# Linear attention on one core: stores behind loads, eps matmuls of 32 rows, head 0 in halves, a new order of work

## The chip, the cores and the metric

The kernel runs on one core of a Trainium2 chip. The metric is the device time of one execution in microseconds (us), lower is better. Repeated runs of one kernel mostly lie within 0.5% of their median. The span that a profile shows is about 1.8 us shorter than the time of the same run.

The engines are called PE or TensorE (matmul; PEld is its weight load), DVE or VectorE, ACT or ScalarE, and POOL or GpSimd. The sync engine SP issues the transfers (DMA).

## The reference

```python
B, H, S, D = 1, 32, 2048, 128          # q, k, v in bfloat16
phi_q = where(q > 0, q + 1, exp(q)) + 1e-6
phi_k = where(k > 0, k + 1, exp(k)) + 1e-6
kv  = einsum("bhsd,bhse->bhde", phi_k, v)
z   = einsum("bhsd->bhd", phi_k)
num = einsum("bhqd,bhde->bhqe", phi_q, kv)
den = einsum("bhqd,bhd->bhq", phi_q, z)[..., None] + 1e-6
return num / den
```

The kernel writes phi(x) as the sum of two parts, min(exp(x), 1) + 1e-6 and relu(x), and lets TensorE add the two by accumulating a matmul of each. A column of ones beside v gives z with kv, so that one 128x129 result per tile holds a numerator and its denominator.

## The kernel before

Each head h has these named pieces of work. Every engine runs its pieces in a fixed order that is written in the program:

- `ek`, `eq`: exp of k and of the transposed q, on ACT. `em`, `emq`: min with 1 and + 1e-6, on VectorE.
- `rk`: relu of k, on VectorE. `rqa`, `rqb`: relu of q, half on ACT and half on VectorE. In every fourth head (`RELU_Q = "SSSA"`) ACT does it all.
- `v1`: a copy of v beside the column of ones, on POOL. `T`: 16 transposes of q on TensorE.
- `kx`, `kv`: 32 matmuls for kv, and `kvs`: its copy from PSUM by ACT.
- `nB`, `nA`, `nC`: the numerator and denominator, 32 matmuls in six PSUM banks, two banks to a group.
- `rA`, `fA`, `rC`, `fC`: reciprocal and multiply on VectorE, 12 tiles and 4 tiles. Then the store.

The 1e-6 in the denominator (called eps here) comes from one small matmul for each bank. A matrix of ones times three columns that sum to eps opens the bank's accumulation:

```python
def numerator(e, h, tiles):                       # one bank: two or three tiles
    s = h % 2
    e.matmul(_ap(o_ps[:, :], SLOT[tiles[0]] + D, [[NC, len(tiles)]]), lhsT=ones[:], rhs=epsr[:, 0:len(tiles)],
             start=True, stop=False, skip_group_check=True)
    for t in tiles:
        o = o_ps[:, SLOT[t]:SLOT[t] + NC]
        e.matmul(o, lhsT=emq_sb[:, s, t * P:(t + 1) * P], rhs=kvs_sb[:, s, :], start=False, stop=False, ...)
        ins = e.matmul(o, lhsT=rq_sb[:, s, t * P:(t + 1) * P], rhs=kvs_sb[:, s, :], start=False, stop=True, ...)
    return ins
# ... cut ...
# num(which, h, banks): for b in banks: numerator(e, h, BANKS[b])
```

Loads and stores are issued in one order by SP. There are eight input buffers and six output buffers:

```python
NI = 8; NO = 6; LAG = 2
for h in range(NH + LAG - 1):
    if h + NI < NH:
        loads(h + NI)
    if h >= LAG:
        store(h - LAG)
```

## Time and profile before

| | before |
|---|---|
| time, median | 180.02 us (3 runs, 179.67 to 180.59; 180.22 with a fourth, timed beside the changed kernel) |
| span of the profiled run | 177.9 us |
| busy: PE, DVE, ACT | 163.9, 155.8, 161.2 us |
| multiply of 12 tiles (`fA`): head 3 to head 23 | 38.52 to 136.78 us, 4.91 us a head |

The first view is the head of the profile's page: busy time, share of the span and instructions of each engine.

```profile
span 177.9 us, 6326 instructions
PE 163.9 (92%) x2822; PEld 157.7 (89%) x2822; DVE 155.8 (88%) x230; ACT 161.2 (91%) x140; POOL 33.1 (19%) x37
```

The second view is the table of busy time by stretch. A line gives the stretch and its length in us, then busy us (and instructions) of PE, PEld, DVE, ACT and POOL, the granted TensorE clock, the DMA share (a sum of packet times, which can come out above 1) and GB/s.

```profile
0.00:20.00 20.00, 15.20 (x201) 14.43 (x202) 8.52 (x20) 13.15 (x11) 2.93 (x8) 0.91 0.91 346
40.00:140.00 100.00, 99.13 (x1762) 96.13 (x1759) 97.57 (x139) 99.75 (x84) 20.82 (x20) 1.00 1.03 415
```

In the middle three engines and the DMA are all nearly full. Which of them binds is told by the chain of waits, the work that ended last followed back step by step. These are its pieces from 59 to 65 us (start, length, what):

```profile
58.92 1.77 ACT la L394
60.69 0.91 ACT la L399
61.60 0.17 ACT la L373
61.77 1.80 ACT la L347
63.57 1.77 ACT la L394
```

The chain runs through ACT without a gap: exp of k (L347), exp of q (L394), half a relu (L399), the copy of kv (L373). That is 4.65 us a head, and 5.5 where ACT does the whole relu. From 40 to 140 us ACT makes up 71% of the chain; VectorE has 13%, and one wait for an outgoing transfer 14%. PE's busy figure of 99% is no evidence of a bound. The records of matmuls overlap: those of full ones are 0.22 us long but start 0.05 to 0.06 us apart, as the timeline of TensorE at an eps matmul (L277) shows:

```profile
60.63 0.22 PE L281 MATMUL la<-la 128*128 128x129 bf16 x1
60.68 0.22 PE L283 MATMUL la<-la 128*128 128x129 bf16 x1
60.74 0.17 PE L277 MATMUL la<-la 128*128 128x3 bf16 x1
60.77 0.22 PE L281 MATMUL la<-la 128*128 128x129 bf16 x1
```

The weight loads (PEld) of the same matmuls follow each other as closely, the one for the eps matmul too:

```profile
60.63 0.10 PEld L283 LDWEIGHTS la<-la 128*128 128x128 bf16 x1
60.69 0.10 PEld L277 LDWEIGHTS la<-la 128*128 128x128 bf16 x1
60.74 0.10 PEld L281 LDWEIGHTS la<-la 128*128 128x128 bf16 x1
```

Read the starts and not the lengths. A full matmul takes 0.057 us from start to start, an eps matmul 0.03. By starts TensorE needs 1.85 us (kv) + 0.89 (transposes) + 1.97 (numerator with six eps matmuls) = 4.7 us a head, which is 0.2 less than the 4.9 us that a head takes.

### The profile page before, as it was taken

To read this page: it belongs to the slowest core of one execution; us is meant where nothing else is said; L and a number is where in the kernel's file an instruction comes from. 1 tells how busy PE (TensorE), PEld (TensorE's weight loads), DVE (VectorE), ACT (ScalarE), POOL (GpSimd) and SP (SyncE) were. 2 spreads that over 40 slices of the span, in tenths; PEclk is the share of its full clock that TensorE was granted. 3 is DMA by queue.
4 is the path that set the end of the run, shared out by engine and by line. 5 is a ranking of instruction groups with operands and counts; after the bars stand their busy time and mean duration, and the time that the engine had idled before them with its cause. 6 is when DMAs were issued, how large, how long until landed. Compare 5 with 4: busy or idle time off the path is not lost.

```text
span 177.9 us, 6326 instructions
## 1 busy us (share of the span) xinstructions
PE 163.9 (92%) x2822; PEld 157.7 (89%) x2822; DVE 155.8 (88%) x230; ACT 161.2 (91%) x140; POOL 33.1 (19%) x37
## 2 busy tenths in 40 slices
PE   6849987999999999999999999999999899999981
PEld 6848886999999999999998999989999799999971
DVE  1255699799999999999999999999999899999983
ACT  5396999989999999999999999999999989996572
POOL 1022022222121222222121122222222022222000
PEclk9996999999999999999999999999999999999998
DMA  5999999999999999999999999999999999984336
GB/s 156 366 417 412 410 407 411 406 410 404 414 415 416 416 413 416 418 412 421 414 411 420 415 418 416 415 419 415 415 416 415 420 413 420 411 333 179 125 122 236
DMA packets 18891, 67.52 MB, mean 380 GB/s; under 512 B 2096, under 2 KB 2480, under 8 KB 18864
## 3 DMA queue, kind: packets, MB, share of 16 engines
q1 hardware_dynamic: 18720, 66.99, 93.7%
q8 instruction: 22, 0.36, 0.8%
q10 hardware_dynamic: 144, 0.13, 0.2%
q14 instruction: 5, 0.04, 0.1%
HBM read 50.33 MB, written 16.78 MB: 377 GB/s over the span
## 4 chain that ended last, share of the span: by engine, by line
ACT 48%; PE 20%; DVE 16%; DMA 12%; issue 1%; SPq 0%; DVEq 0%
ACT la L347 19%; ACT la L394 18%; PE la L362 9%; DMA out_dram<-la 9%; ACT la L399 8%; DVE la L307 8%; PE la L281 4%; PE la L283 3%; PE la L354 3%; DMA la<-in_q_dram 3%; ACT la L373 2%; DVE la L339 2%; DVE la L402 2%; DVE la L406 2%; DVE la L303 1%
## 5 line engine op out<-in xcount | busy, mean ns | idle before, releaser
L307 DVE TENSOR_TENSOR la<-la 128x512 bf16<-128x512 f32 (+2 forms) x64 | 77.2, 1206 | 3.7 <-DMA out_dram<-la 1.2
L283 PE MATMUL la<-la 128*128 128x129 bf16 x512 | 68.0, 220 | 0.0
L281 PE MATMUL la<-la 128*128 128x129 bf16 x512 | 68.0, 219 | 0.0
L362 PE MATMUL la<-la 128*128 128x129 bf16 x1024 | 65.5, 222 | 0.6 <-DVE la L307 0.5
L394 ACT ACTIVATE la<-la 128x2048 bf16<-128x2048 bf16 x31 | 58.8, 1895 | 5.1 <-PE la L354 3.0
L347 ACT ACTIVATE la<-la 128x2048 bf16<-128x2048 bf16 (+1 forms) x33 | 61.7, 1877 | 1.4 <-DMA la<-in_k_dram 1.4
L362 PEld LDWEIGHTS la<-la 128*128 128x128 bf16 x1024 | 61.3, 99 | 1.2 <-DVE la L307 0.8
L378 POOL COPY la<-la 128x1024 int32<-128x1024 int32 x31 | 32.4, 1046 | 128.7 <-DVE la L303 115.1
L283 PEld LDWEIGHTS la<-la 128*128 128x128 bf16 x512 | 49.5, 97 | 0.0
L281 PEld LDWEIGHTS la<-la 128*128 128x128 bf16 x512 | 47.1, 97 | 0.0
L399 ACT ACTIVATE la<-la 128x1024 bf16<-128x1024 bf16 (+1 forms) x31 | 38.5, 1241 | 0.0
L277 PE MATMUL la<-la 128*128 128x3 bf16 (+1 forms) x192 | 32.5, 169 | 5.1 <-DVE la L307 3.0
L354 PE MATMUL la<-la 128*128 128x128 bf16 x512 | 33.9, 219 | 3.0 <-DVE la L402 2.1
L354 PEld LDWEIGHTS la<-la 128*128 128x128 bf16 x512 | 29.6, 98 | 4.4 <-DVE la L402 3.2
L277 PEld LDWEIGHTS la<-la 128*128 128x128 bf16 x192 | 18.7, 97 | 9.1 <-DVE la L307 7.1
L406 DVE TENSOR_SCALAR la<-la 128x2048 bf16<-128x2048 bf16 x31 | 21.1, 682 | 5.8 <-ACT la L394 5.8
L339 DVE TENSOR_SCALAR la<-la 128x4096 bf16<-128x4096 bf16 (+1 forms) x18 | 19.8, 1100 | 3.0 <-DMA la<-in_k_dram 3.0
L331 DVE TENSOR_SCALAR la<-la 128x4096 bf16<-128x4096 bf16 (+1 forms) x18 | 19.8, 1098 | 1.0 <-ACT la L347 0.9
L402 DVE TENSOR_SCALAR la<-la 128x1024 bf16<-128x1024 bf16 x24 | 16.1, 673 | 2.1 <-ACT la L394 2.1
L303 DVE RECIPROCAL la<-la 128x4 f32<-128x4 f32 (+2 forms) x66 | 13.1, 200 | 2.9 <-PE la L283 2.6
L373 ACT ACTIVATE la<-la 128x129 bf16<-128x129 f32 x32 | 9.6, 301 | 3.1 <-PE la L362 1.6
L437 PE MATMUL la<-la 128*128 128x120 bf16 x70 | 6.2, 273 | 1.5 <-POOL la L222 1.5
(18 smaller groups left out, 16.1 us busy)
## 6 DMA issues: line engine op xcount, KB each, us to landing
la<-in_q_dram SPq DMA_DIRECT2D x32, 512.0 KB, 15.4
la<-in_v_dram SPq DMA_DIRECT2D x32, 512.0 KB, 15.8
la<-in_k_dram SPq DMA_DIRECT2D x31, 512.0 KB, 15.3
out_dram<-la SPq DMA_DIRECT2D x31, 512.0 KB, 15.2
la<-in_k_dram SPq DMA_DIRECT2D x2, 256.0 KB, 2.9
out_dram<-la SPq DMA_DIRECT2D x2, 192.0 KB, 2.1
out_dram<-la ACTq DMA_DIRECT2D x1, 128.0 KB, 1.9
```

What stands on the lines that cost most here:

```text
L277: e.matmul(_ap(o_ps[:, :], SLOT[tiles[0]] + D, [[NC, len(tiles)]]), lhsT=ones[:], rhs=epsr[:, 0:len(tiles)], start=True, stop=False, skip_ ...
L281: e.matmul(o, lhsT=emq_sb[:, s, t * P:(t + 1) * P], rhs=kvs_sb[:, s, :], start=False, stop=False, skip_group_check=True)
L283: ins = e.matmul(o, lhsT=rq_sb[:, s, t * P:(t + 1) * P], rhs=kvs_sb[:, s, :], start=False, stop=True, skip_group_check=True)
L307: add("DVE", f"f{which}{h}", lambda e: e.tensor_tensor(out=_ap(o_sb[:, :, :, :], ob + t0 * D, [[n * D, nb], [D, n], [1, D]]), in0=_ap(o_ps ...
L339: add("DVE", key, lambda e: e.tensor_scalar(rk_sb[:, s:s + n], k_sb[:, b:b + n], 0.0, None, op0=ALU.max), [d for i in range(n) for d in ld ...
L347: add("ACT", "ek0.0" if h == 0 and r == 0 else f"ek{h}", lambda e, c=c: e.activation(em_sb[:, h % 4, c], k_sb[:, h % NI, c], ACT.Exp), ([f ...
L354: ins = e.transpose(xT[:, j * P:(j + 1) * P], q_sb[:, h % NI, j * D:(j + 1) * D], ident[:])
L362: ins = e.matmul(kv_ps, lhsT=src[:, h % 4, j * D:(j + 1) * D], rhs=v1_sb[:, h % 2, j, 0:NC], start=(j + part == 0), stop=(j == NT - 1 and ...
L378: add("DVE" if h < V1_DVE else "POOL", f"v1{h}", lambda e, h=h, s=s: e.tensor_copy(v1_sb[:, s, :, 0:D].bitcast(i32), v_sb[:, h % NI].rearr ...
L394: add("ACT", f"eq{h}", lambda e, s=s: e.activation(emq_sb[:, s], xT[:, :], ACT.Exp), [f"T{h}"] + nums(h - 2))
L399: add("ACT", key, lambda e, s=s, c=c: e.activation(rq_sb[:, s, c], xT[:, c], ACT.Relu), [f"T{h}"] + nums(h - 2))
L406: add("DVE", f"emq{h}", lambda e, s=s: e.tensor_scalar(emq_sb[:, s], emq_sb[:, s], 1.0, EPS, op0=ALU.min, op1=ALU.add), [f"eq{h}"])
```

## The change

It means to let the input run ahead of the output, to shorten the start, to make the eps matmuls cheaper by giving them 32 rows instead of 128, and to order all engines' work anew. The diff, cut to its core (the long lists of the order are left out):

```diff
-    NO = 6
+    NO = 12
-    LAG = 2
+    LAG = [2+h//3 for h in range(40)]      # stores: 2 heads behind the loads, later 9
-    WARM1 = 22
+    WARM1 = 40
+    WARM2 = 8
+    HALF = "kq"                            # head 0: q too is loaded, transposed, exponentiated in halves
-    RELU_Q = "SSSA" * (NH // 4)
+    RELU_Q = "S" * 32                      # relu of q always half on ACT, half on VectorE
     # ... SCHEDULE: every engine's order replaced ...
-    a = bf(EPS / 128)                      # eps pieces: sums over 128 rows, now over 32
+    a = bf(EPS / 32)
-        def numerator(e, h, tiles):
+        def numerator(e, h, banks):
             s = h % 2
-            e.matmul(_ap(o_ps[:, :], SLOT[tiles[0]] + D, [[NC, len(tiles)]]), lhsT=ones[:], rhs=epsr[:, 0:len(tiles)],
-                     start=True, stop=False, skip_group_check=True)
-            for t in tiles:
+            for b in banks:
+                r, n = slice(32 * (b % 4), 32 * (b % 4) + 32), len(BANKS[b])
+                e.matmul(_ap(o_ps[:, :], SLOT[BANKS[b][0]] + D, [[NC, n]]), lhsT=ones[r, :], rhs=epsr[r, 0:n],
+                         start=True, stop=False, skip_group_check=True)
+            for t in [t for b in banks for t in BANKS[b]]:
-        for h in range(NH + LAG - 1):
-            if h + NI < NH:
-                loads(h + NI)
-            if h >= LAG:
-                store(h - LAG)
+        done = 0
+        for h in range(NH - NI):
+            loads(h + NI)
+            while done <= h - LAG[h]:
+                store(done)
+                done += 1
+        for h in range(done, L):
+            store(h)
```

So each group of two banks now begins with a pair of 32-row eps matmuls, each on its own 32 of the 128 rows (the profile writes them 32*128, the full ones 128*128), followed by 8 or 12 full matmuls. There are 96 such places in the kernel.

## The prediction

> **What bounds it now.** In the middle everything is nearly full: busy time by stretch, 60 to 80 us, has ACT 20.00 of 20, DVE 19.48, PE 19.84, DMA at 415 GB/s. Four heads take 19.62 us (VectorE timeline, 45.13 to 64.75), 4.9 us a head. Needs per head, from issue intervals in the timelines: ACT 1.80+1.77+0.91+0.17 = 4.65 us, and 5.5 where it does the whole relu of q (every fourth head), mean 4.86; DVE 4.87; PE 1.85 (kv) + 0.89 (transposes) + about 1.97 (numerator, with six eps matmuls at 0.03) = 4.7; DMA 2.1 MB at 416 GB/s = 5.04. So the middle is ACT and DVE in balance, with DMA close behind. The ends are loose: VectorE works 8.5 us of the first 20, TensorE's clock is 0.78 between 10 and 15 us. From 140 us on VectorE waits for stores (0.88 and 0.29 us; a store takes 15 us to land, six output buffers), and DMA falls to 116-195 GB/s after 160 us.
>
> **What changes.**
> 1. Seven heads' relu goes from ACT-only to split: ACT drops to 4.65 a head, VectorE gains 7 x 0.6 us, plus 0.7 for the last head: about +5 us of VectorE work. VectorE then needs 5.02 us a head and is the only binding engine in the middle.
> 2. Later stores and 12 buffers take away store waits, about 1.5 us of VectorE; loads end some 12 us earlier, but little waited for them.
> 3. Head 0 in halves and more warm-up: first transpose near 6.3 instead of 7.0, first kv product at the full clock (1.85 instead of 3.5 us). It still can't outrun v1's landing (12.25 us by the POOL copy's wait). Counting VectorE work done, I estimate a gain of about 4 us by 20 us.
> 4. The eps matmuls cost 0.03 x 192 = 5.8 us of TensorE in all; with 32 rows perhaps half. TensorE has slack. [...] Three groups a head: if a group cost over 0.15 us, TensorE would become the bound.
> 5. The new order should keep VectorE fed, and at the end (relu of head 31 on VectorE beside ACT) remove most of its last idle time.
>
> **Sum.** VectorE busy 155.8 + 5 = 160.8 us, about 1.5 us of small bubbles, 8.4 us idle at the start, 2.6 us from the last multiply to the end, 2 us of fill and tail waits: span 175.3 us; the profiled run was 1.74 us above its span, so **177.0 us** (-1.7%). Range 173.5 to 180.0. Faster by over 2%: 0.45, within 2%: 0.50, slower: 0.05.
>
> **Signs.** VectorE busy near 161 us and over 97% from 20 to 165 us; ACT busy near 155 with gaps; VectorE four-head period 20.0 to 20.2 us; the chain of waits in the middle on VectorE lines rather than ACT's; no VectorE multiply waiting on an outgoing DMA; loads' last landing near 143 us with stores drained after; TensorE's clock above 0.9 between 10 and 15 us; the first large multiply issued near 17.5 instead of 22.9 us.
>
> **What would make it wrong.** [...] VectorE idling 4 us or more in the middle because the in-order queues interlock (178-180). Or VectorE's small bubbles shrinking by interleaving reciprocals and other work, and less than 7 us lost at the start (173-175).

The sum came to 160.8 + 1.5 + 8.4 + 2.6 + 2 = 175.3 us of span, 177.0 us of time.

## The result, and the profile after

The changed kernel took 185.64 us (median of 4, 184.91 to 186.18). The ratio to before is 1.0301, 95% interval 1.0248 to 1.0353: 3% slower.

The head of the page:

```profile
span 184.3 us, 6420 instructions
PE 174.8 (95%) x2848; PEld 161.6 (88%) x2848; DVE 162.7 (88%) x251; ACT 156.3 (85%) x139; POOL 32.9 (18%) x37
```

The table of busy time by stretch, with the columns as above:

```profile
40.00:140.00 100.00, 98.70 (x1623) 91.04 (x1621) 95.10 (x136) 93.18 (x79) 18.67 (x18) 1.00 1.03 414
```

ACT now has 7% of gaps and VectorE 5%, so neither of them holds the middle. From 40 to 140 us TensorE makes up 83% of the chain of waits. Some of its pieces (again start, length, what):

```profile
62.05 1.84 PE la L414 x32
63.88 0.89 PE la L404 x16
64.78 0.11 PE la L304 x2
64.89 0.16 PE la L308
65.05 0.06 PE la L310
```

The timeline of TensorE at an eps pair (L304), and below it that of the weight loads around the same place:

```profile
81.16 0.22 PE L308 MATMUL la<-la 128*128 128x129 bf16 x1
81.22 0.22 PE L310 MATMUL la<-la 128*128 128x129 bf16 x1
81.37 0.18 PE L304 MATMUL la<-la 32*128 32x2 bf16 x2
81.48 0.23 PE L308 MATMUL la<-la 128*128 128x129 bf16 x1
81.55 0.22 PE L310 MATMUL la<-la 128*128 128x129 bf16 x1
```

```profile
81.11 0.10 PEld L308 LDWEIGHTS la<-la 128*128 128x128 bf16 x1
81.16 0.10 PEld L310 LDWEIGHTS la<-la 128*128 128x128 bf16 x1
81.36 0.09 PEld L304 LDWEIGHTS la<-la 32*128 32x128 bf16 x2
81.47 0.10 PEld L308 LDWEIGHTS la<-la 128*128 128x128 bf16 x1
```

From the last full matmul (81.22) to the next (81.48) pass 0.26 us. Without anything between them it would be 0.057, so the pair costs about 0.20 us of TensorE, where two eps matmuls of 128 rows cost 0.06. This place is no exception: over all pairs from 20 to 170 us in the trace the median is 0.26 us from full matmul to full matmul. The weight loads show how. Between full matmuls a load starts about one step (0.05 us) before its matmul, while the record of the matmul in front still runs. The load of the eps pair starts only 0.01 us before its matmul, 0.20 us after the load in front of it (between full loads it is 0.056), and the next full load starts in the same way only 0.01 us before its own, 0.11 us after the pair's. The profile names hardly anything that they waited for: of 11.4 us of idle time before the eps loads it puts 1.6 down to other engines (in the kernel before, 8.8 of 9.1).

Three places a head cost about 3 x 0.14 = 0.43 us more, so TensorE's need rises from 4.7 to about 5.14 us a head. The starts of the transposes, once a head, came at 63.72, 68.93 and 74.12 us, 5.20 us apart. (VectorE's `fA` from head 4 at 40.69 to head 22 at 137.07 us gives 5.35. That is more than a head takes, because the new order moves `nA` back meanwhile: from just after the next head's transposes, `T5 nA4`, to after its kv as well, `T23 kx23 kv23 nC22 nA22`.) TensorE had become the bound.

### The profile page after: what moved, and what is told of

It reads as the page before. It is cut to its first block, busy times and chain, and to the rows that moved or that the text cites. A ratio compares the mean times of both kernels' runs of the same rounds, so it can differ in the third digit from the quotient of the medians.

```text
span 184.3 us, 6420 instructions
## 1 busy us (share of the span) xinstructions
PE 174.8 (95%) x2848; PEld 161.6 (88%) x2848; DVE 162.7 (88%) x251; ACT 156.3 (85%) x139; POOL 32.9 (18%) x37
## 4 chain that ended last, share of the span: by engine, by line
PE 77%; DVE 10%; DMA 6%; ACT 5%; issue 1%; SPq 0%; DVEq 0%
PE la L414 27%; PE la L308 19%; PE la L310 14%; PE la L404 13%; DVE la L331 6%; PE la L304 5%; DMA la<-in_q_dram 4%; ACT la L444 3%; DMA la<-in_k_dram 1%; DVE la L360 1%; ACT la L398 1%; DVE la L457 1%; DVE la L328 1%; DVE la L452 1%; ACT la L449 0%
## 5 line engine op out<-in xcount | busy, mean ns | idle before, releaser
L444 ACT ACTIVATE la<-la 128x2048 bf16<-128x2048 bf16 (+1 forms) x32 | 58.4, 1825 | 15.5 <-PE la L404 15.4
L398 ACT ACTIVATE la<-la 128x2048 bf16<-128x2048 bf16 (+1 forms) x33 | 61.3, 1860 | 2.0 <-DMA la<-in_k_dram 2.0
L414 PEld LDWEIGHTS la<-la 128*128 128x128 bf16 x1024 | 59.9, 97 | 1.4 <-ACT la L421 0.5
L310 PEld LDWEIGHTS la<-la 128*128 128x128 bf16 x512 | 50.2, 98 | 0.0
L308 PEld LDWEIGHTS la<-la 128*128 128x128 bf16 x512 | 47.7, 97 | 1.5
L404 PEld LDWEIGHTS la<-la 128*128 128x128 bf16 x512 | 29.9, 98 | 2.9 <-DMA la<-in_q_dram 1.6
L449 ACT ACTIVATE la<-la 128x1024 bf16<-128x1024 bf16 x31 | 31.6, 1020 | 0.0
L457 DVE TENSOR_SCALAR la<-la 128x2048 bf16<-128x2048 bf16 (+1 forms) x32 | 20.8, 650 | 4.2 <-ACT la L444 4.2
L452 DVE TENSOR_SCALAR la<-la 128x1024 bf16<-128x1024 bf16 x31 | 21.1, 680 | 3.7 <-ACT la L444 3.6
L304 PEld LDWEIGHTS la<-la 32*128 32x128 bf16 x192 | 9.0, 90 | 11.4 <-DVE la L331 1.1
L304 PE MATMUL la<-la 32*128 32x3 bf16 (+1 forms) x192 | 17.0, 173 | 0.9 <-DVE la L331 0.8
L360 DVE TENSOR_SCALAR la<-la 128x4096 bf16<-128x4096 bf16 x14 | 17.1, 1218 | 0.2
L391 DVE TENSOR_SCALAR la<-la 128x4096 bf16<-128x4096 bf16 x14 | 16.9, 1209 | 0.0
L421 ACT ACTIVATE la<-la 128x129 bf16<-128x129 f32 x32 | 9.0, 282 | 1.3 <-PE la L310 0.6
L488 PE MATMUL la<-la 128*128 128x120 bf16 x96 | 7.1, 250 | 1.5 <-POOL la L231 1.5
```

The lines of the kernel that those rows point to most:

```text
L304: e.matmul(_ap(o_ps[:, :], SLOT[BANKS[b][0]] + D, [[NC, n]]), lhsT=ones[r, :], rhs=epsr[r, 0:n], start=True, stop=False, skip_group_check= ...
L398: add("ACT", key, lambda e, c=c: e.activation(em_sb[:, h % 4, c], k_sb[:, h % NI, c], ACT.Exp), l + o + [prev("kv", h, 4)])
L404: ins = e.transpose(xT[:, j * P:(j + 1) * P], q_sb[:, h % NI, j * D:(j + 1) * D], ident[:])
L414: ins = e.matmul(kv_ps, lhsT=src[:, h % 4, j * D:(j + 1) * D], rhs=v1_sb[:, h % 2, j, 0:NC], start=(j + part == 0), stop=(j == NT - 1 and ...
L444: add("ACT", key, lambda e, s=s, c=c: e.activation(emq_sb[:, s, c], xT[:, c], ACT.Exp), [f"T{h}{r}"] + o + nums(h - 2))
L449: add("ACT", key, lambda e, s=s, c=c: e.activation(rq_sb[:, s, c], xT[:, c], ACT.Relu), [f"T{h}" + (parts("T", h, "q")[0][4] if RELU_Q[h] ...
```

## The experiments

Theory 1 was this cost of the eps places. Theory 2 was that the new order, with all relu halves on VectorE, is slow by itself. Theory 3 was that late stores cost time. All twelve runs were correct against the reference. Every kernel was timed in three rounds against the kernel before on the same chip. There were three such groups, in which the kernel before had medians of 179.68, 179.94 and 179.82 us (180.22 beside the changed kernel); medians of different groups are therefore compared directly below, and differences under about half a microsecond are not read.

### The eps matmuls back to 128 rows, everything else as changed

```diff
-                r, n = slice(32 * (b % 4), 32 * (b % 4) + 32), len(BANKS[b])
-                e.matmul(..., lhsT=ones[r, :], rhs=epsr[r, 0:n], ...)
+                n = len(BANKS[b])
+                e.matmul(..., lhsT=ones[:], rhs=epsr[:, 0:n], ...)
```

(The pieces of eps and their memsets go back with it.)

> The changed kernel with only the eps matmuls back to 128 rows (one for each bank, two in front of each group as in the change; the order of work is untouched). Theory 1 (a pair of 32-row eps matmuls holds TensorE for 0.20 us where two of 128 rows took 0.06, 96 pairs, 13 us, and makes TensorE the bound at about 5.14 us a head): TensorE falls to 4.72 us a head, VectorE binds at about 5.02 us, time 175 to 179 us. Theory 2 (the new order of work and all relu halves on VectorE make it slow, the eps only shows it): time stays at 183 to 186 us.

Measured: 177.02 us, ratio to before 0.9852 (0.9824 to 0.988). The eps form alone makes 8.6 us between this and the changed kernel. Theory 2 falls as a cause of the slowing. This is TensorE's timeline at a pair, which now takes 0.05 us (90.25 to 90.36, less 0.057):

```profile
90.25 0.22 PE L309 MATMUL la<-la 128*128 128x129 bf16 x1
90.31 0.19 PE L303 MATMUL la<-la 128*128 128x3 bf16 x2
90.36 0.22 PE L307 MATMUL la<-la 128*128 128x129 bf16 x1
```

The table of busy time by stretch shows VectorE as the fullest engine now:

```profile
0.00:20.00 20.00, 16.51 (x248) 16.03 (x249) 9.74 (x25) 14.95 (x13) 2.79 (x8) 1.00 0.90 344
40.00:140.00 100.00, 96.67 (x1710) 93.25 (x1708) 98.19 (x142) 97.09 (x81) 20.52 (x20) 1.00 1.03 414
```

### Only the eps form put into the kernel before

The edit is the change's `numerator` and eps pieces in the kernel before, with its own order, stores and relu split.

> The kernel before with only the eps matmuls changed to the paired 32-row form. Theory 1: TensorE needs 5.14 us a head where ACT and VectorE need 4.87, so the time rises by 6 to 9 us, to 186 to 189 us, and the chain of waits turns from ACT to TensorE. Theory 2: within 1% of 180 us.

Measured: 189.22 us, ratio 1.0515 (1.0446 to 1.0585), so 9.5 us slower. The chain of waits of this run is 84% TensorE by engine. The cost belongs to the eps form and shows in either order of work.

### Only the late stores put into the kernel before

```diff
-    NO = 6
+    NO = 12
-    LAG = 2
+    LAG = [2+h//3 for h in range(40)]
```

(and the loop that issues loads and stores, as in the change)

> The kernel before with only the stores behind the loads and 12 output buffers. Theory 1 (stores are not the cause of the slowing): the waits of VectorE for outgoing DMAs (1.2 us) vanish, time 178 to 180 us. Theory 3 (the late stores cost time, by a backlog or a tail of DMA): 182 us or more.

Measured: 178.37 us, ratio 0.9929 (0.990 to 0.9958). Theory 3 falls: late stores gain 1.3 us. The two waits of VectorE's multiply for an outgoing transfer (1.2 us before) are gone from its table of waits.

### The pair taken apart: twice as many places

```diff
-            for b in banks:
-                <eps matmul of bank b>
-            for t in [t for b in banks for t in BANKS[b]]:
+            for b, t in [(b, t) for b in banks for t in BANKS[b]]:
+                if t == BANKS[b][0]:
+                    <eps matmul of bank b, 32 rows>
```

> The changed kernel with the two 32-row eps matmuls of a group apart, one in front of each bank's tiles: the same matmuls, twice as many changes between 128 and 32 rows. Theory 1 (the change of rows costs, about 0.14 to 0.17 us each): 192 places instead of 96, 13 to 16 us more, 197 to 202 us. If a 32-row matmul is itself slow (0.1 us each, whatever its neighbours), the time stays at 185 to 187 us.

Measured: 204.7 us, ratio 1.1385 (1.1357 to 1.1412). The matmuls are the same in number and shape as in the changed kernel, but the time is 19.1 us longer, which is 0.20 us for each of the 96 added places. The forecast of 197 to 202 us was too low, because it put an added place at 0.14 to 0.17 us. A single eps matmul is no cheaper than a pair. This is TensorE's timeline there:

```profile
81.72 0.22 PE L310 MATMUL la<-la 128*128 128x129 bf16 x1
81.87 0.17 PE L305 MATMUL la<-la 32*128 32x3 bf16 x1
81.98 0.23 PE L308 MATMUL la<-la 128*128 128x129 bf16 x1
```

One eps matmul takes the same 0.26 us from full matmul to full matmul (81.72 to 81.98) as two. What is paid for is the place and not the matmul. In the pairs of the changed kernel the second matmul starts 3 to 4 ns after the first, so it adds next to nothing. Nor does it matter which rows the small matmul takes: the eps matmuls of two columns, half of which use rows 0 to 31, and those of three columns all take 0.26 us here.

### Four eps matmuls in one place: fewer places

```diff
-            for b in banks:
+            for b in eps_at(which, h, banks):      # first of A and B: banks 0 to 3; the other: none
```

> The changed kernel with 32-row eps matmuls, but the four of banks 0 to 3 in one place of each head (the first of its two groups), four row groups side by side: 66 places instead of 96, the same 192 matmuls. If the place costs and not the matmul: 30 x 0.2 = 6 us less TensorE, which comes to about 4.95 us a head, just under VectorE's 5.02, so 178 to 181 us. If the matmul costs: 184 to 187 us.

Measured: 181.45 us, ratio 1.009 (1.0068 to 1.0112), 4.2 us less than the changed kernel for 30 places fewer; the forecast said 178 to 181, and all four runs lie just above it. That is 0.14 us a place, less than 0.20. From 40 to 140 us the chain of waits is 62% TensorE and 24% VectorE, against 83% and 14% in the changed kernel, so part of the bound has passed to VectorE. That does not explain all of it: the run is still 4.4 us slower than the one with 128 rows, though the forecast's 4.95 us of TensorE a head should fit under VectorE's 5.02. What holds the rest is not shown. Four matmuls in one place take no longer than two, in TensorE's timeline (here TensorE had waited for data in front of them, so only what follows can be read):

```profile
79.05 0.18 PE L310 MATMUL la<-la 32*128 32x3 bf16 x4 [0.17 <-DVE la L463]
79.16 0.23 PE L314 MATMUL la<-la 128*128 128x129 bf16 x1
```

It is 0.11 us from the first of the four to the next full matmul, as for the pair (81.37 to 81.48) and for a single one (81.87 to 81.98). Over the 24 such places of the trace without a wait, from 20 to 170 us, the median from full matmul to full matmul is 0.27 us.

### 96 rows and 64 rows

```diff
-   lhsT=ones[32*(b%4):32*(b%4)+32, :]
+   lhsT=ones[0:96, :]                      # one run
+   lhsT=ones[64*(b%2):64*(b%2)+64, :]      # another run
```

> The changed kernel with eps matmuls of 96 rows. Theory 1a [...]: same as 128 rows, 176.5 to 178 us, a pair takes 0.06 us. Theory 1b (any eps matmul with fewer rows than its neighbours is held up): 184 to 187 us, a pair takes 0.2 us.

Measured with 96 rows: 176.75 us, ratio 0.9823 (0.977 to 0.9876), the same as with 128 rows. TensorE's timeline:

```profile
85.38 0.22 PE L309 MATMUL la<-la 128*128 128x129 bf16 x1
85.44 0.20 PE L303 MATMUL la<-la 96*128 96x3 bf16 x2
85.49 0.22 PE L307 MATMUL la<-la 128*128 128x129 bf16 x1
```

Here the pair takes 0.05 us. Fewer rows are not what costs.

> The changed kernel with eps matmuls of 64 rows (two row halves), in pairs as in the change. [...] 64 rows cost the same as 32, 184 to 187 us. If only 32 rows are hit: 176.5 to 178 us.

Measured with 64 rows: 185.69 us, ratio 1.0333 (1.0309 to 1.0357), the same as with 32. In its timeline of TensorE a pair takes 0.26 us from full matmul to full matmul (81.04 to 81.30), as with 32 rows.

So 32 and 64 rows cost and 96 and 128 do not: a pair takes 0.26 us from full matmul to full matmul with the former, 0.11 with the latter. With 32 rows a place takes 0.26 to 0.27 us in the timeline whether one, two or four small matmuls lie in it. Why these row counts cost is not shown by any run. What the trace shows is that weight loads stop running ahead at such a place: over the changed kernel's places from 20 to 170 us a 32-row load starts 0.20 us (median) after the load in front of it, against 0.056 between full ones. That the small matmul uses rows which its full neighbours use too can't by itself be the reason: 96 rows do as well, and their pair takes 0.05 us.

### What the rest of the change is worth

These five start from the changed kernel with 128-row eps (177.02 us).

Without any eps matmul (wrong by 1e-6 in the denominator):

```diff
-            for b in banks:
-                <eps matmul of bank b>
+            # none; the first matmul of each bank has start=True
```

> The changed kernel without any eps matmul (wrong on purpose by 1e-6 in the denominator, which bf16 does not show): takes all 192 eps matmuls from TensorE. If TensorE is no bound once the eps have 128 rows: 176.3 to 177.3 us, the same as with 128-row eps. If TensorE still matters: up to 5.8 us faster, 171 to 174 us.

Measured: 176.54 us, ratio to before 0.9822 (0.9766 to 0.9877). That is 0.5 us less than with them, and the single runs overlap. TensorE was hardly a bound any more: even if 32 rows had been free, cheaper eps matmuls could have gained about half a microsecond at most.

Stores as before (two heads behind, six buffers):

```diff
-    NO = 12
+    NO = 6
-    LAG = [2+h//3 for h in range(40)]
+    LAG = [2] * 40
```

> The changed kernel with 128-row eps, and stores as before (two heads behind, 6 output buffers). From the run of late stores on the kernel before (1.3 us gained): 178 to 179.5 us. If the new order of work depends on the late stores: 181 us or more. If late stores gain nothing here: 176.5 to 177.5 us.

Measured: 180.22 us, ratio to before 1.0024 (0.9974 to 1.0074), a little above the forecast. In the new order the late stores are worth 3.2 us; without them its gain is gone. ACT's exp of k then waits for its load 11 times, 4.9 us in all (3 times, 1.9 us, with late stores).

The relu of q of heads 3, 7, ... 27 back on ACT alone:

```diff
-    RELU_Q = "S" * 32
+    RELU_Q = "SSSA" * 7 + "SSSS"           # and rqb3, rqb7, ... rqb27 out of VectorE's order
```

> The changed kernel with 128-row eps, and in addition the relu of q of heads 3, 7, ... 27 back on ACT alone (7 half relus of 0.6 us taken from VectorE). If VectorE is the bound that is left (5.02 us a head): 4 us less VectorE work, 173 to 175 us. If memory traffic (2.1 MB a head at 415 GB/s, 5.04 us) or the order of work holds it: 176.5 to 178 us, or slower, as the order was made for the other split.

Measured: 181.94 us, ratio to before 1.0114 (1.0068 to 1.016). Seven half relus less on VectorE made it 4.9 us slower: VectorE is busy 92.26 of the 100 us from 40 to 140 us instead of 98.19, and ACT 96.97. This is the miss among the expectations that teaches most: taking work from the fullest engine, without a new order, opened gaps in it. The likely reason, which the expectation names but no run isolates, is that the order was made for the other split. So this run does not tell what that split could reach with an order of its own.

Head 0's q whole, and the warm-up of before:

```diff
-    WARM1 = 40
-    WARM2 = 8
-    HALF = "kq"
+    WARM1 = 22
+    WARM2 = 0
+    HALF = "k"                             # and T0.0, eq0.0, emq0.0 and warm2 out of the orders
```

> The changed kernel with 128-row eps, with q of head 0 loaded, transposed and exponentiated whole, and the warm-up of before (22 matmuls after the first transpose, none after). If the halves and the warm-up bring the 1 to 2 us that VectorE's work by 20 us shows (9.7 us done against 8.5 before): 178 to 179.5 us. If other waits at the start hide them: 176.5 to 177.5 us.

Measured: 176.95 us, ratio to before 0.9842 (0.9809 to 0.9874), no difference. The half of q that comes last decides: exp of the second half started at 8.73 us, when exp of the whole q started at 8.04 us without halves, and ACT's next piece began at 9.65 against 9.81 us. VectorE even did more by 20 us without the halves, 10.81 us of work against 9.74.

A try for a better version, a quarter of k's relu on POOL:

```diff
-    RKP = [()]*32
+    RKP = [()]*4 + [((12, 16),)]*28        # tiles 12 to 15 of k's relu, and rkp4 ... rkp31 into POOL's order
```

> A try for a better version: the changed kernel with 128-row eps, and a quarter of k's relu (4 of 16 tiles, heads 4 to 31) moved from VectorE to POOL, which is 19% busy. VectorE then needs about 4.88 us a head instead of 5.02. If VectorE alone is the bound: 173 to 175 us. If memory traffic (5.04 us a head at 415 GB/s) or the order of work is as close: 176 to 178 us. If POOL's work slows VectorE's or comes late: over 178 us.

Measured: 178.62 us, ratio to before 0.9928 (0.9904 to 0.9951), 1.6 us slower than without. VectorE's relu of a pair of heads fell from 1.21 to 1.04 us, but its mins of k (1218 to 1336 ns) and of q (665 to 733 ns) grew, and its busy time rose from 159.6 to 160.8 us. These are groups by line (busy us, mean ns) of the run with 128-row eps and of this one, the min of k (L359, here L358):

```profile
L359 DVE TENSOR_SCALAR la<-la 128x4096 bf16<-128x4096 bf16 x14 | 17.1, 1218 | 0.3 <-ACT la L397 0.2
```

```profile
L358 DVE TENSOR_SCALAR la<-la 128x4096 bf16<-128x4096 bf16 x14 | 18.7, 1336 | 0.2 <-ACT la L396 0.2
L365 POOL TENSOR_SCALAR la<-la 128x512 int16<-128x512 int16 x10 | 17.7, 1783 | 0.8 <-DMA la<-in_k_dram 0.8
```

The longer mins go with POOL's work, and the trace goes one step further than the mean: of the 14 mins of k, the 7 that ran while POOL was idle took 1210 to 1228 ns as before; of the 7 that overlapped a POOL instruction, 5 took 1353 to 1722. VectorE's half relus of q, which read PSUM, did not grow (675 against 681 ns). Why those mins took longer is not shown by any run.

The best version is therefore the changed kernel with its eps matmuls at 128 or 96 rows, about 177 us, 1.5 to 1.8% under the kernel before.

## Why the prediction was wrong

The prediction of 177.0 us (173.5 to 180.0) missed 185.64. The step that failed is number 4: "The eps matmuls cost 0.03 x 192 = 5.8 us of TensorE in all; with 32 rows perhaps half. TensorE has slack." A pair was thus taken at about 0.03 us and measured 0.20. Over 96 places TensorE pays 13 to 14 us more than for 128 rows, 0.43 us a head, against a slack of 0.2 to 0.3 us. The same step even worked out a threshold ("if a group cost over 0.15 us, TensorE would become the bound"). Yet the sum was written as if the group cost nothing, and "slower" got 5%. A cost that no run had measured stood against a thin slack, and that deserved far more than the tail of the range.

The other terms, judged by the run with 128-row eps (177.02 us), in which only this step is undone:

- **The middle** (step 1) held in its size. VectorE was 98.19% busy from 40 to 140 us. The transposes of heads 5 to 24 came 4.98 us apart (35.99 to 130.61 us), against a predicted need of 5.02 and 4.89 before (`fA` of heads 4 to 23, 39.60 to 136.81 us, gives 5.12 for the reason told above), and at 137 us both kernels were at the same head 23. But VectorE was not "the only binding engine": the chain of waits from 40 to 140 us is 35% VectorE, 34% ACT and 28% TensorE.
- **The late stores** (step 2) were predicted at about 1.5 us. They gave 1.3 us on the kernel before and 3.2 us in the new order. "Little waited for" the loads was wrong for the new order, where ACT waits for k when stores come early.
- **The start** (step 3) was over-estimated. VectorE did 9.74 us of work by 20 us instead of 8.52, idle 10.3 us where 8.4 were predicted. The first large multiply began at 19.77 us (before 22.93, predicted 17.5; the runs with early stores, with ACT's whole relus and with POOL's relu, whose order up to there is the same, had it at 18.59, 18.86 and 19.04, so one trace tells it to about 1 us). Halves and warm-up brought none of it (the run with q whole); what remains for it is the new order, which no run here isolates. TensorE's clock did rise as predicted, from 0.78 to 1.00 between 10 and 15 us, but runs of the kernel before with a mean clock of 1.000 and of 0.987 took 179.44 and 179.46 us, so the dip costs nothing that can be seen.
- **The end** (step 5) was better than thought. From `fA` of head 23 at about 137 us to the end of the span it takes 38.5 us with the new parts and 41.1 us before. It is here that the version with 128-row eps gains, as the lead of the start is spent in the middle.

That the sum came out at 177.0 against 177.02 is partly luck: too short a start (1.9 us in the one trace) was made up for by less VectorE work than reckoned (159.6 busy against 160.8) and fewer waits later.

## What to carry to other kernels

Do not scatter matmuls of 32 or 64 rows in a stream of 128-row ones: they cost 0.2 us a place here, more than three full matmuls (0.057 us each). Put them in fewer places (30 places fewer saved 4.2 us), or use 96 or 128 rows (0.05 us a pair). Before one makes an operation cheaper, ask whether its engine binds; removing these matmuls altogether gained 0.5 us. And an order of work tuned for one split of the work is not neutral to another split: taking work off the fullest engine without a new order made the kernel slower.
